# Transposing the half block, pairing two attends, reversing tiles and a shorter ring in a sparse attention with gated FFN

## The chip, the cores and the metric

One core of a Trainium2 chip. The time is the device time of one launch in microseconds (us), the median of the runs shown. A profile is one execution recorded by the hardware profiler.

## The reference

Eight batches, eight heads, 576 tokens, head dimension 64. Scores within `tau` of a row's maximum are kept, the others leave the softmax. The result, 512 columns wide, goes through a feed-forward layer of width 1024 with a convolution over three neighbouring tokens as its gate.

```python
scores = scale * np.matmul(q, k.transpose(0, 1, 3, 2))
thresh = np.max(scores, axis=-1, keepdims=True) - tau
scores = np.where(scores >= thresh, scores, -1000000000.0)
attn = np.exp(scores - np.max(scores, axis=-1, keepdims=True))
attn = attn / (np.sum(attn, axis=-1, keepdims=True) + 1e-09)
x = np.matmul(attn, v)                  # heads side by side: (8, 576, 512)
h = np.maximum(x @ w_in, 0.0)           # (8, 576, 1024)
conv_out[s] = sum(conv_w[k] * h[s + k - 1] for k in range(3))
gate = 1.0 / (1.0 + np.exp(-conv_out))
out = h * gate @ w_out                  # (8, 576, 512)
```

All is float32. The weights `w_in`, `w_out` and `conv_w` come as 64-bit words.

## The kernel before

**Tiles.** Heads go in four pairs a batch. The 576 query rows of a batch are five tiles: four of 128 rows and one half tile of 64. A *chunk* is two tiles (0, 1) or three (2, 3, 4) of a batch, so there are 16 chunks, 64 combinations of chunk and head pair, and 160 units (a unit is one tile of one pair).

**A unit** (`unit`, L421) computes scores into PSUM (`ps_s`): for batches after the first with full rows and q and k each split into a high and a low float32r part (L449, all 128 rows of the array); for the first batch, and for the half tiles of every batch, in plain float32 with the array cut into halves by rows (L442). In a half tile both heads share the 128 partitions. DVE takes the row maximum (L457) and masks and sums (L466), ACT takes the exponential (L463), small instructions on DVE or POOL work out threshold and inverse (L460, L483, L487, L490), and POOL normalizes (L495). The result is `em`, 128 x 1152, in four buffers.

**Transposes** (`transposes`, L500) turn `em` block by block on TensorE into `ps_t` (L519, two PSUM buffers); ACT copies it to `eT` (L514, one buffer). 576 keys are four blocks of 128 and a half block of 64. For full tiles the half blocks of both heads are one block of 128 columns. For a half tile the half block is done by `halves` (L532): two matmuls against parts of the identity, each for one head, which put head 0 on partitions 0 to 63 and head 1 on 64 to 127 (L534).

**Attend** (`attend`, L562) multiplies `eT` by v for one pair, two heads at a time, each on half of the array's columns (L571), into `pa`, which takes a buffer of the tag `ps_t` as the transposes do. ACT and DVE copy it as high and low part to `x` (L579, L582).

**FFN** (`ffn`, L677). `mm1` (L588) does one eighth of the hidden width for a chunk (L600), then ReLU, the three taps (L618, L627), tanh and gate (L634), and writes the result in two parts to a ring of 640 tokens. `mm2` (L656) multiplies 128 tokens of the ring by `w_out` (L665). The work of a chunk's `mm1` and of the `mm2` of the tokens that were finished by the chunk before is spread over the units of the next chunk; one `mm2` alternates with two `mm1`.

**Order.** Nothing is issued in program order. `Plan.op` collects every instruction group with an engine, a price in ns, what it reads and writes, and a rank (the unit's number less an `ahead`). `Plan.run` simulates the engines with those prices, `LATENCY` between engines and `SWITCH` between kinds of matmul ("rows", "cols", "turn", "full"), and issues for each engine the ready group of lowest rank; TensorE may stay with a kind that costs under 50 ns to follow within `KEEP` ranks. A group with `other` may go to another engine when its own has more than `BACKLOG` ready; there it is ranked `ALT` later. The buffers of a tag are handed out in the order in which the program made them. The order so found is fixed in the kernel: each engine and SP's queue of loads run it strictly in turn.

**Weights** are loaded and taken apart (`split`, L295) over the first some twenty units, at a pace set by `WRATE`.

Of the kernel before, what the change touches and what calls it, by code (L numbers as in the profile page):

```python
# [61 lines left out]
class Plan:  # L62
# [13 lines left out]
    def op(self, engine, ns, fn, w=(), r=(), ahead=0.0, other=None, kind=None):  # L76
# [12 lines left out]
        bufs = {x[0] for x in (*w, *r)}  # L89
        for x in bufs:  # L90
            x.left += 1
        self.ops.append((((engine, ns), *(other or ())), self.rank - ahead, fn if other is not None else lambda e: fn(), before, bufs, kind))

    def run(self):
# [28 lines left out]
        while events:  # L123
            t = events[0][0]
            while events and events[0][0] <= t:
                _, _, kind, x = heapq.heappop(events)
                if kind == "ready":
                    i, e = x
                    if taken[i] is None:
                        heapq.heappush(ready[e], (self.ops[i][1] + (0.0 if e == self.ops[i][0][0][0] else ALT), i))  # L130
                        if e == self.ops[i][0][0][0]:
                            load[e] += self.ops[i][0][0][1]
                elif kind == "release":
                    live.discard(x)
                elif kind == "done":
                    engine = taken[x]
                    for j in after[x]:
                        waits[j] -= 1
                        for e in came[j]:
                            late = 0.0 if e == engine == "pe" else LATENCY[engine] + (30.0 if e == "pool" != engine else 0.0)  # L140
# [66 lines left out]
def tile_tau_attention_gated_ffn(  # L207
# [54 lines left out]
    op("sp", 100, lambda: nc.sync.dma_start(tau_sb[:], tau.broadcast_to([P, 1])), w=[(tau_sb, 0)], ahead=100.0)  # L262
# [19 lines left out]

    def act(n, psum=False):
        return n * 0.833 + (170 if psum else 200)

    def dve(n, fixed=140):
        return n * 1.1 + fixed

    def pool(n):
        return n * 2.1 + 240  # L290

    def pool1(n):
        return n * 1.69 + 80

    def split(src, n, name, high, low, hr, lr, queue="sp"):  # L295
# [37 lines left out]
        op(queue, 450, load, w=[hi, lo], ahead=w + (AHEAD["load"] if queue == "sp" else 90))  # L333
        op("act", act(n), f0, w=[a], r=[hi], ahead=w)
        op("pool", n * 1.69 + 80, f1, w=[a], ahead=w, other=[("dve", 150 + n * 0.65)])
        op("dve", 150 + n * 0.55, f2, w=[a], ahead=w)
        op("dve", 150 + n * 1.1, f3, w=[a], r=[hi], ahead=w)
        op("dve", 150 + n * 1.1, f4, w=[a], r=[lo], ahead=w)
# [32 lines left out]
    RING = 5 * P  # L371
# [10 lines left out]
    def prep_rows(i, b, p, o, w, tag):  # L382
# [4 lines left out]
        op("sp", 450, lambda: nc.sync.dma_start(k[:], kp[b, p]), w=[(k, 0)], ahead=a + 2)  # L387
        op("sp", 450, lambda: nc.sync.dma_start(q[:], qd[b, p, :, :, o:o + w]), w=[(q, 0)], ahead=a + 2)
        op("act", act(2 * w), lambda: nc.scalar.activation(q[:], q[:], AF.Copy, scale=0.125), w=[(q, 0)], ahead=a)
        return k, q  # L390

    def prep_k(b, p, j, ks):
# [3 lines left out]
        op("sp", 820, lambda: nc.sync.dma_start(xk[:, :S], kd[b, p, :, j]), w=[(xk, 0)], ahead=a + 2)  # L396
# [7 lines left out]
    def prep_q(i, b, p, j, q1, q2):  # L404
# [4 lines left out]
        op("sp", 455, lambda: nc.sync.dma_start(xq[:], qd[b, p, :, j, o:o + w]), w=[(xq, 0)], ahead=a + 2)  # L409
# [6 lines left out]
    def load_v(i, b, p):  # L416
        vt = plan.buf(wk, "v", 2, [P, NBLK + 1, D], F32, f"v_{i}")
        op("sp", 820, lambda: nc.sync.dma_start(vt[:], vc[b, p]), w=[(vt, 0)], ahead=AHEAD["prep"])
        return vt

    def unit(u, k, q1, q2, o, n):  # L421
# [9 lines left out]
        tiny = [("pool", 290)]  # L431
        for h, js in enumerate(heads):
# [26 lines left out]
            def limit(e, nm=nm, th=th):  # L459
                engines[e].tensor_scalar(few[:rows, th], few[:rows, nm], -1.0, tau_sb[:rows], op0=ALU.mult, op1=ALU.subtract)  # L460
# [4 lines left out]
            def mask(ps=ps, th=th, view=view, total=total):  # L465
# [6 lines left out]
                "pe", 480 if q2 is None else 532, mm, w=[(ps, 0)],  # L472
                r=[(k, 0), (q1, 0)] if q2 is None else [(x, h) for x in (k, q1, q2)], ahead=a, kind="rows" if q2 is None else "full"
            )
            op("dve", 748, top, w=[(few, ("nm", h))], r=[(ps, 0)], ahead=a)
            op("act", 742, exp, w=[(em, h)], r=[(ps, 0), (few, ("nm", h))], ahead=a)
            op("dve", 200, limit, w=[(few, ("th", h))], r=[(few, ("nm", h)), (tau_sb, 0)], ahead=a, other=tiny)
            op("dve", 890, mask, w=[(em, h), (few, ("sum", h))], r=[(ps, 0), (few, ("th", h))], ahead=a)
# [10 lines left out]
        op("dve", 170, guard, w=[(few, "inverse")], r=ss, ahead=a, other=tiny)  # L489
        op("dve", 160, lambda: nc.vector.reciprocal(few[:rows, inverse], few[:rows, inverse]), w=[(few, "inverse")], ahead=a)  # L490
        op("dve", 165, even, w=[(few, "shift")], r=ss, ahead=a, other=tiny)
        for h in range(m):
            def norm(e, h=h):
                sl = em[:rows, h * S:(h + 1) * S]
                engines[e].tensor_scalar(sl, sl, few[:rows, 6 + h:7 + h], few[:rows, 8 + h:9 + h], op0=ALU.mult, op1=ALU.add)  # L495

            op("pool", 905, norm, w=[(em, h)], r=[(few, "inverse"), (few, "shift")], ahead=a, other=[("dve", 490)])
        return em

    def transposes(u, ems, tiles, eT):  # L500
# [4 lines left out]
        def group(i, reads, parts, *evacs):  # L505

            pt = plan.buf(ps_t, "ps_t", 2, [P, 512], F32, f"ps_t_{u}_{i}")
            width = sum(w for w, _, _ in evacs)
            op(
                "pe", max(width, 140) * 0.86, lambda: parts(pt), w=[(pt, 0)], r=reads + [(ident, 0)], ahead=AHEAD["t"], kind="turn"  # L510
# [7 lines left out]
        def turn(pt, at, em, b):  # L518
            nc.tensor.transpose(out=pt[:, at:at + P], in_=em[:, b * P:(b + 1) * P], identity=ident[:])  # L519
# [11 lines left out]

        def halves(pt, at):  # L532
            for j in range(2):
                nc.tensor.matmul(  # L534
                    pt[j * D:(j + 1) * D, at:at + n], lhsT=em[:, 4 * P:4 * P + D], rhs=ident[:, j * n:(j + 1) * n], start=True, stop=True
                )

# [10 lines left out]
        full = [x for x in ems if x[1] == P]  # L548
# [11 lines left out]
        group(8, [(x[0], 1) for x in full] + ([(em, 0)] if n < P else []), odd, *parts)  # L560

    def attend(i, eT, vt, w, x, off):  # L562
        pa = plan.buf(ps_t, "ps_t", 2, [P, 512], F32, f"pa_{i}")
        parts = [x for x in plan.wrote if x[0] is eT]
        for r in range(5):
# [10 lines left out]
            op("pe", w * 4 / 2.4 + 20, mm, w=[(pa, 0)], r=parts + [(vt, 0)], ahead=AHEAD["a"], kind="cols")  # L576
# [11 lines left out]
    def mm1(c, f, xs):  # L588
# [8 lines left out]
        for cb in range(NCB):  # L597
# [8 lines left out]
            op("pe", an * 3 / 2.4 + 40, mm, w=[(ph, 0)], r=ws + [(xs[cb], i) for i in (0, 1, 2) if i < 2 or a0], kind="full")  # L606
# [17 lines left out]
        op("pool", pool1(kn), tap0, w=[(t, 0)], r=[(hp, 0), (cw, 0)], other=[("dve", dve(kn / 2, 130))])  # L624
        for k in (0, 2):
# [5 lines left out]
            op("dve", dve(kn, 300), tap, w=[(t, 0)], r=[(hp, 0), (hp, 1), (cw, 0)])  # L631
# [24 lines left out]
    def mm2(m):  # L656
# [5 lines left out]
        for f in range(NFB):  # L662
# [8 lines left out]
            op("pe", 695, mm, w=[(po, 0)], r=gs + [(w, (f, i)) for w in w2 for i in range(0, DO, WN)], kind="full")  # L671
        op("act", act(DO, True), lambda: nc.scalar.activation(ot[:, :DO], po[:], AF.Copy), w=[(ot, 0)], r=[(po, 0)])
        op("sp", 730, lambda: nc.sync.dma_start(tokens[m * P:(m + 1) * P, :], ot[:, :DO]), r=[(ot, 0)])
# [3 lines left out]
    def ffn(c):  # L677
# [8 lines left out]
        if c < EARLY:  # L686
            return first + second
        while first or second:
# [4 lines left out]
    xs = {}  # L693
    pairs = [(c, p) for c in range(len(chunks)) for p in range(NP)]
    units = [(i, t) for i in range(len(pairs)) for t in chunks[pairs[i][0]].tiles]
# [30 lines left out]
    work = []  # L726
    for now in range(len(units) + 1):
        plan.rank = float(now)
        if now < len(units):
            i, t = units[now]  # L730
            c, p = pairs[i]
            tiles, (o, w), (a0, an) = chunks[c].tiles, chunks[c].new, chunks[c].cols
# [7 lines left out]
            if t == tiles[-1]:  # L740
# [9 lines left out]
                attend(i, eT, vts[i], w, x, off)  # L750
# [65 lines left out]
```

## Time and profile before

| | |
|---|---|
| median of 3 runs | 976.28 us (975.6 to 979.25) |
| profiled execution, its own time | 977.8 us |
| its span, first to last instruction | 976.0 us |
| TensorE busy (matmul) | 925.7 us, 6368 matmuls |
| DVE, POOL, ACT busy | 804.6, 728.6, 694.8 us |
| mean granted TensorE clock | 0.990 |
| bytes moved | 87.26 MB, mean 89 GB/s |

In the lists of instructions a row has engine, line, operation, the tiles written and read, the shapes, a count, the busy time and the mean duration of one, and after the bar the idle time of the engine ahead of them with what ended it. In a timeline a row is the start, the time until the last of its merged instructions ended, engine, line and count. Matmuls overlap, so a step is read from one start to the next. In the list of waits a row has the time in all, how often, and the longest.

### The profile page before, as it was taken

The numbers are of one execution on the slowest core, as the hardware profiler recorded it, in microseconds if no ns is written. First come the engines' busy times: TensorE is split into PE (matmuls) and PEld (weight loads), VectorE is DVE, ScalarE is ACT, GpSimd is POOL, SyncE is SP. The second block draws the span as 40 slices with busy tenths as digits, with TensorE's granted clock in tenths as the row PEclk, the third lists the DMA queues.
The fourth block names the chain that finished last, engine by engine and source line by source line (L and its number), as shares of the span: only waits on it lengthen the run. The fifth ranks groups of instructions, "written<-read, shape, count | busy, mean of one in ns | idle before, by whom it ended". The sixth has DMA issues, their size and how long they took to land.

```text
span 976.0 us, 19384 instructions
## 1 busy us (share of the span) xinstructions
PE 925.7 (95%) x6368; PEld 740.6 (76%) x6368; DVE 804.6 (82%) x1926; ACT 694.8 (71%) x1508; POOL 728.6 (75%) x1175
## 2 busy tenths in 40 slices
PE   3887779999999999999999999999999999999998
PEld 2554558878888878878888788887888878887796
DVE  4889989997988887887897879897897879988443
ACT  4766778777876778767876678777876778776443
POOL 3769898876888678887886769886776877786333
PEclk9999989999999999999999999999999999999999
DMA  6344223233322133213332223223332133311000
GB/s 224 122 146 142 80 85 115 73 91 98 94 93 80 61 104 112 85 53 105 99 106 63 81 84 108 86 74 95 104 99 76 52 102 109 100 50 46 23 22 33
DMA packets 56259, 87.26 MB, mean 89 GB/s; under 512 B 13152, under 2 KB 29536, under 8 KB 56160
## 3 DMA queue, kind: packets, MB, share of 16 engines
q1 hardware_dynamic: 55728, 84.46, 28.5%
q10 hardware_dynamic: 432, 1.57, 0.5%
q8 instruction: 51, 0.84, 0.4%
q14 instruction: 48, 0.39, 0.1%
HBM read 76.57 MB, written 9.44 MB: 88 GB/s over the span
## 4 chain that ended last, share of the span: by engine, by line
PE 74%; DVE 10%; POOL 7%; issue 3%; DMA 2%; ACT 2%; SPq 0%; POOLq 0%; DVEq 0%; ACTq 0%
PE ph L600 17%; PE po L665 17%; PE pa L571 13%; PE ps_t L519 12%; PE ps_s L449 11%; PE ps_s L442 3%; DVE em L466 3%; POOL em L495 3%; DMA q<-in_qd_dram 2%; DVE few L457 2%; POOL gl L280 2%; DVE t L627 1%; DVE t L634 1%; POOL t L618 1%; PE ps_t L534 1%
## 5 line engine op out<-in xcount | busy, mean ns | idle before, releaser
L495 POOL TENSOR_SCALAR em<-em,few 128x576 f32<-128x576 f32 x288 | 263.5, 922 | 42.4 <-DVE few L490 29.3
L466 DVE SCALAR_TENSOR_TENSOR em<-ps_s,few,em 128x576 f32<-128x576 f32 x288 | 230.1, 811 | 36.3 <-ACT em L463 30.2
L457 DVE TENSOR_REDUCE few<-ps_s 128x1 f32<-128x576 f32 x288 | 212.9, 750 | 56.1 <-PE ps_s L449 39.4
L600 PE MATMUL ph<-x,w1h 128*128 128x322 f32 (+1 forms) x1024 | 251.8, 309 | 0.9 <-ACT hp L615 0.6
L463 ACT ACTIVATE em<-ps_s,few 128x576 f32<-128x576 f32 x288 | 209.0, 740 | 42.0 <-DVE few L457 31.5
L514 ACT ACTIVATE eT<-ps_t 128x512 f32<-128x512 f32 (+2 forms) x384 | 193.8, 532 | 48.0 <-PE ps_t L519 44.8
L519 PE MATMUL ps_t<-ident,em 128*128 128x128 f32 x1280 | 191.5, 279 | 12.0 <-POOL em L495 8.1
L627 DVE SCALAR_TENSOR_TENSOR t<-hp,cw,t 128x255 f32<-128x255 f32 (+1 forms) x256 | 176.6, 693 | 29.8 <-POOL t L618 28.1
L519 PEld LDWEIGHTS ps_t<-ident,em 128*128 128x128 f32 x1280 | 148.9, 142 | 52.3 <-POOL em L495 17.4
L600 PEld LDWEIGHTS ph<-x,w1h 128*128 128x128 f32 x1024 | 177.5, 190 | 7.9 <-issue 3.9
L571 PE MATMUL pa<-eT,v 128*64 128x256 f32 (+1 forms) x1280 | 171.5, 415 | 0.0
L449 PE MATMUL ps_s<-ks,q 128*128 128x288 f32 x896 | 159.4, 306 | 7.8 <-DVE em L466 3.2
L600 PE MATMUL ph<-x,w1l 128*128 128x322 f32 (+1 forms) x512 | 152.1, 297 | 0.0
L449 PEld LDWEIGHTS ps_s<-ks,q 128*128 128x128 f32 x896 | 131.2, 189 | 23.3 <-issue 7.4
L571 PEld LDWEIGHTS pa<-eT,v 128*64 128x64 f32 x1280 | 87.1, 138 | 67.3 <-issue 7.5
L280 POOL TENSOR_TENSOR gl<-t,gh 128x321 fp32r<-128x321 f32 (+13 forms) x184 | 119.3, 660 | 12.2 <-ACT gh L644 10.6
L665 PE MATMUL po<-w2h,gh 128*128 128x512 f32 x288 | 118.4, 411 | 0.0
L665 PE MATMUL po<-w2h,gl 128*128 128x512 f32 x288 | 113.7, 395 | 2.2 <-POOL gl L280 2.2
L665 PE MATMUL po<-w2l,gh 128*128 128x512 f32 x288 | 113.3, 393 | 0.0
L618 POOL TENSOR_SCALAR t<-hp,cw 128x321 f32<-128x321 f32 (+1 forms) x128 | 71.9, 562 | 38.2 <-ACT hp L615 31.3
L600 PEld LDWEIGHTS ph<-x,w1l 128*128 128x128 f32 x512 | 97.3, 190 | 0.3
L280 POOL TENSOR_TENSOR ks<-xk,ks 64x576 fp32r<-64x576 f32 x56 | 81.7, 1460 | 16.5 <-ACT ks L398 10.2
(56 smaller groups left out, 1127.6 us busy)
## 6 DMA issues: line engine op xcount, KB each, us to landing
v<-in_vc_dram SPq DMA_DIRECT2D x64, 320.0 KB, 3.0
xk<-in_kd_dram SPq DMA_DIRECT2D x56, 288.0 KB, 2.9
xq<-in_qd_dram SPq DMA_DIRECT2D x112, 128.0 KB, 2.3
k<-in_kp_dram SPq DMA_DIRECT2D x36, 320.0 KB, 3.1
out_dram<-ot SPq DMA_DIRECT2D x36, 256.0 KB, 2.0
stage<-in_w_out_dram SPq DMA_DIRECT2D x8, 512.0 KB, 3.4
stage<-in_w_in_dram SPq DMA_DIRECT2D x5, 512.0 KB, 4.1
q<-in_qd_dram SPq DMA_DIRECT2D x28, 64.0 KB, 3.2
```

Of the source, the lines that this page charges most:

```text
L280: engines[e].tensor_tensor(dst, x, y, op=ALU.subtract)
L449: nc.tensor.matmul(ps[:, c, :CH], lhsT=q[:, h, o:o + n], rhs=k[:, h, c * CH:(c + 1) * CH], start=(i == 0), stop=(i == 1))
L457: nc.vector.tensor_reduce(few[:rows, nm], ps[:rows, :, :CH], op=ALU.max, axis=mybir.AxisListType.XY, negate=True)
L463: nc.scalar.activation(view(), ps[:rows, :, :CH], AF.Exp, bias=few[:rows, nm])
L466: nc.vector.scalar_tensor_tensor(view(), ps[:rows, :, :CH], few[:rows, th], view(), op0=ALU.is_ge, op1=ALU.mult, accum_out=few[:rows, total])
L495: engines[e].tensor_scalar(sl, sl, few[:rows, 6 + h:7 + h], few[:rows, 8 + h:9 + h], op0=ALU.mult, op1=ALU.add)
L514: "act", act(w, True), lambda dst=dst, src=src: nc.scalar.activation(dst(), src(pt), AF.Copy),
L519: nc.tensor.transpose(out=pt[:, at:at + P], in_=em[:, b * P:(b + 1) * P], identity=ident[:])
L571: nc.tensor.matmul(pa[j * D:(j + 1) * D, :w], lhsT=vt[:, blk + j, :], rhs=eT[:, blk, :w], start=(r == 0), stop=(r == 4))
L600: nc.tensor.matmul(ph[:, :an], lhsT=w1[w][:, cb, fs], rhs=xs[cb][:, h, :an], start=(cb == 0 and i == 0), stop=(cb == NCB - 1 and i == 2))
L627: nc.vector.scalar_tensor_tensor(t[:, :kn], hp[:, k:kn + k], cw[:, 3 * f + k:3 * f + k + 1], t[:, :kn], op0=ALU.mult, op1=ALU.add)
L665: nc.tensor.matmul(po[:], lhsT=x[:, f, at:at + P], rhs=w[:, f, :], start=(f == 0 and i == 0), stop=(f == NFB - 1 and i == 2))
```

## The change

- **Half block as a transpose.** `halves` goes. The last group of a chunk's pair transposes columns 448 to 575 of the half tile's `em` as one block more (`turn(..., 3.5)`); the keys wanted lie on partitions 64 to 127 of the result, and two ACT copies of 64 x 64 take them to `eT`, one for each head.
- **v for two pairs.** From chunk 3 on (`JOINT = 3`) the attend of an even pair waits for that of the odd pair behind it: both are issued when the parts of both are there. `eT` has two buffers.
- **Tiles in reverse** for each odd pair (`order`), so that half tiles of two pairs are neighbours.
- **Ring of 512 tokens** in place of 640. In `ffn` all `mm2` of the chunk before stand ahead of the `mm1`.
- **Start.** The first k is loaded from ACT's queue ahead of its weight loads, the first q heads SP's queue; q of the first batch is scaled in two instructions.
- The threshold is taken with a negated `tau` and may go to ACT too, as may the normalization.
- **The planner's numbers:** `AHEAD`, `LATENCY`, `SWITCH`, `KEEP`, `ALT`, `BACKLOG`, `WRATE` and most prices, those of loads by their size; a group may have a delay of its own (`late`).

```diff
-AHEAD = {'s': 6.0, 't': 3.5, 'a': 3.5, 'prep': 4.0, 'w': 2.0, 'load': 4.25}
-LATENCY = {"pe": 197.0, "act": 145.0, "dve": 130.0, "pool": 115.0, "sp": 2000.0}
+AHEAD = {'s': 6.0, 't': 3.25, 'a': 3.0, 'prep': 4.0, 'w': 2.75, 'load': 4.75}
+LATENCY = {"pe": 210.0, "act": 145.0, "dve": 110.0, "pool": 75.0, "sp": 2000.0}
-MOE = (2, 1)
-BACKLOG = {'pool': 28000.0, 'dve': 500.0, 'act': 9000000000.0}
-WRATE = (0.891, 1.015)
-ALT = 3.0
+MOE = (2, 2)
+BACKLOG = {'pool': 28000.0, 'dve': 343.0, 'act': 9000000000.0}
+WRATE = (0.891, 0.894)
+ALT = 12.0
...
-    "rows": {"cols": 190, "turn": 240, "full": 290}, "cols": {"rows": 230, "turn": 260, "full": 310},
-    "turn": {"rows": 95, "cols": 95, "full": 85}, "full": {"rows": 95, "cols": 95, "turn": 5},
+    "rows": {"cols": 145, "turn": 155, "full": 200}, "cols": {"rows": 205, "turn": 155, "full": 205},
+    "turn": {"rows": 195, "cols": 145, "full": 5}, "full": {"rows": 195, "cols": 145, "turn": 0},
 }
-KEEP = 1.2
+JOINT = 3
+KEEP = 2.352
...
-    RING = 5 * P
+    RING = 4 * P
...
-        op("sp", 450, lambda: nc.sync.dma_start(k[:], kp[b, p]), w=[(k, 0)], ahead=a + 2)
-        op("sp", 450, lambda: nc.sync.dma_start(q[:], qd[b, p, :, :, o:o + w]), w=[(q, 0)], ahead=a + 2)
+        if i:
+            op("sp", sp(S + D), lambda: nc.sync.dma_start(k[:], kp[b, p]), w=[(k, 0)], ahead=a + 2)
+        else:
+            op("act", 450, lambda: nc.scalar.dma_start(k[:], kp[b, p]), w=[(k, 0)], ahead=210, late=sp(S + D) + LATENCY["sp"])
+        op("sp", sp(2 * w), lambda: nc.sync.dma_start(q[:], qd[b, p, :, :, o:o + w]), w=[(q, 0), (q, 1)], ahead=a + 2 + 100 * (not i))
...
-        def halves(pt, at):
-            for j in range(2):
-                nc.tensor.matmul(
-                    pt[j * D:(j + 1) * D, at:at + n], lhsT=em[:, 4 * P:4 * P + D], rhs=ident[:, j * n:(j + 1) * n], start=True, stop=True
-                )
...
         def odd(pt):
-            for i, x in enumerate(full):
-                turn(pt, i * P, x[0], 8)
-            if n < P:
-                halves(pt, w)
+            for x in full + small:
+                turn(pt, x[2], x[0], 8 if x[1] == P else 3.5)
 
         parts = [(w, lambda: eT[:, 8, :w], lambda pt: pt[:, :w])]
-        if n < P:
-            parts.append((n, lambda: eT[:, 4, off:off + n], lambda pt: pt[:, w:w + n]))
+        for _, m, at in small:
+            for j in range(2):
+                parts.append((
+                    m, lambda j=j: eT[j * D:(j + 1) * D, 4, at:at + m], lambda pt, j=j: pt[D:, w + j * m:w + (j + 1) * m]
+                ))
...
         if c < EARLY:
             return first + second
+        while len(second) > 1:
+            seq.append(second.pop(0))
         while first or second:
             seq += second[:n2] + first[:n1]
             first, second = first[n1:], second[n2:]
...
+    def order(i):
+        c, p = pairs[i]
+        return chunks[c].tiles[::-1] if p % 2 else chunks[c].tiles
...
-                eT = plan.buf(wk, "eT", 1, [P, NBLK, 320], F32, f"eT_{i}")
+                eT = plan.buf(wk, "eT", 2, [P, NBLK, 320], F32, f"eT_{i}")
...
-                attend(i, eT, vts[i], w, x, off)
+                parts = [x for x in plan.wrote if x[0] is eT]
+                waiting.append((i, eT, vts[i], w, x, off, parts))
+                if c < JOINT or p % 2:
+                    parts = [x for y in waiting for x in y[-1]]
+                    for y in waiting:
+                        attend(*y[:-1], parts)
+                    waiting = []
```

More of the change, by code (lines that the diff above doesn't have):

```diff
@@ L74, in buf, with op @@
         return b
-    def op(self, engine, ns, fn, w=(), r=(), ahead=0.0, other=None, kind=None):
+    def op(self, engine, ns, fn, w=(), r=(), ahead=0.0, other=None, kind=None, late=0.0):
         i = len(self.ops)
@@ L91, in op @@
             x.left += 1
-        self.ops.append((((engine, ns), *(other or ())), self.rank - ahead, fn if other is not None else lambda e: fn(), before, bufs, kind))
+        self.ops.append((((engine, ns), *(other or ())), self.rank - ahead, fn if other is not None else lambda e: fn(), before, bufs, kind, late))
     def run(self):
@@ L139, in run @@
                         for e in came[j]:
-                            late = 0.0 if e == engine == "pe" else LATENCY[engine] + (30.0 if e == "pool" != engine else 0.0)
+                            late = 0.0 if e == engine == "pe" else LATENCY[engine] + self.ops[x][6] + (60.0 if e in ("pool", "pe") and e != engine else 0.0)
                             came[j][e] = max(came[j][e], t + late)
@@ L331, in f4 @@
             nc.vector.scalar_tensor_tensor(v(U32), words()[0], 29, v(U32), op0=ALU.logical_shift_right, op1=ALU.bitwise_or)
-        op(queue, 450, load, w=[hi, lo], ahead=w + (AHEAD["load"] if queue == "sp" else 90))
+        if queue == "sp":
+            op("sp", sp(2 * n), load, w=[hi, lo], ahead=w + AHEAD["load"])
+        else:
+            op("act", 450, load, w=[hi, lo], ahead=90, late=sp(2 * n) + LATENCY["sp"])
         op("act", act(n), f0, w=[a], r=[hi], ahead=w)
[L335 to L338, printed above, removed]
+        op("pool", 600 * n / 512, f1, w=[a], ahead=w, other=[("dve", 150 + n * 0.65)])
+        op("dve", 70 + n * 0.53, f2, w=[a], ahead=w)
+        op("dve", 100 + n * 1.3, f3, w=[a], r=[hi], ahead=w)
+        op("dve", 100 + n * 1.3, f4, w=[a], r=[lo], ahead=w)
         op("act", act(n), lambda: nc.scalar.activation(high(), v(), AF.Copy), w=[hr], r=[a], ahead=w)
@@ L430, in unit @@
         a = AHEAD["s"]
-        tiny = [("pool", 290)]
+        tiny = [("pool", 200)]
         for h, js in enumerate(heads):
@@ L503, in transposes, with group @@
         em, n, off = ems[-1]
-        def group(i, reads, parts, *evacs):
+        def group(i, reads, parts, *evacs, width=4 * P):
             pt = plan.buf(ps_t, "ps_t", 2, [P, 512], F32, f"ps_t_{u}_{i}")
-            width = sum(w for w, _, _ in evacs)
             op(
-                "pe", max(width, 140) * 0.86, lambda: parts(pt), w=[(pt, 0)], r=reads + [(ident, 0)], ahead=AHEAD["t"], kind="turn"
+                "pe", width * 0.852, lambda: parts(pt), w=[(pt, 0)], r=reads + [(ident, 0)], ahead=AHEAD["t"], kind="turn"
             )
@@ L518, in turn @@
         def turn(pt, at, em, b):
-            nc.tensor.transpose(out=pt[:, at:at + P], in_=em[:, b * P:(b + 1) * P], identity=ident[:])
+            nc.tensor.transpose(out=pt[:, at:at + P], in_=em[:, int(b * P):int(b * P) + P], identity=ident[:])
         def turns(pt, b0):
@@ L693, in tile_tau_attention_gated_ffn @@
     xs = {}
+    def order(i):
+        c, p = pairs[i]
+        return chunks[c].tiles[::-1] if p % 2 else chunks[c].tiles
     pairs = [(c, p) for c in range(len(chunks)) for p in range(NP)]
-    units = [(i, t) for i in range(len(pairs)) for t in chunks[pairs[i][0]].tiles]
+    units = [(i, t) for i in range(len(pairs)) for t in order(i)]
     whole, last, vts = {}, {}, {}
@@ L725, in tile_tau_attention_gated_ffn @@
         load_weight(i)
-    work = []
+    work, waiting = [], []
     for now in range(len(units) + 1):
@@ L731, in tile_tau_attention_gated_ffn @@
             c, p = pairs[i]
-            tiles, (o, w), (a0, an) = chunks[c].tiles, chunks[c].new, chunks[c].cols
+            tiles, (o, w), (a0, an) = order(i), chunks[c].new, chunks[c].cols
             at, n = TILES[t]
```

79 lines of the change are left out of this document (47 added, 32 removed).

## The prediction, before the run

> **What bounds the kernel now.** I read the page's totals first, then the busy time by stage, then TensorE's waits.
>
> ```profile
> span 976.0 us, 19384 instructions
> PE 925.7 (95%) x6368; PEld 740.6 (76%) x6368; DVE 804.6 (82%) x1926; ACT 694.8 (71%) x1508; POOL 728.6 (75%) x1175
> GB/s 224 122 146 142 80 85 115 73 91 98 94 93 80 61 104 112 85 53 105 99 106 63 81 84 108 86 74 95 104 99 76 52 102 109 100 50 46 23 22 33
> ```
>
> TensorE is busy for 95% of the span, DVE for 82%. An average over the span can hide stages with other limits, so the next view cuts it (columns: PE, weight loads, DVE, ACT, POOL, granted clock, DMA share, GB/s).
>
> ```profile
> 0.00:60.00 60.00, 39.56 (x228) 23.22 (x230) 40.72 (x101) 35.09 (x64) 32.88 (x63) 0.95 0.51 166
> 60.00:180.00 120.00, 100.08 (x674) 72.80 (x673) 112.43 (x254) 89.10 (x180) 106.07 (x133) 0.94 0.36 109
> 180.00:930.00 750.00, 744.16 (x5258) 608.50 (x5257) 633.36 (x1545) 554.28 (x1225) 572.24 (x944) 1.00 0.28 84
> ```
>
> There are two stages. Up to 180 us TensorE is idle for 20.4 + 19.9 = 40 us, and from 60 us on DVE is busy for 112 of 120: weights are being split beside the first batch. From 180 to 930 us TensorE is busy for 744 of 750 us at full clock, while DVE, the next engine, has 117 us to spare. In that stage a microsecond taken off TensorE is a microsecond off the time, as long as the others keep up.
>
> ```profile
> PE ps_s L442 <- ACT q L389: 11.2, 1, 11.2
> PE ps_s L449 <- DVE em L466: 2.1, 4, 0.8
> ```
>
> The first row is TensorE's one long wait in the whole trace: its first work, waiting for the first q. The second is its largest in 180 to 930 us, 2.1 us in all. So TensorE hardly waits there, and what can go is its own work. Busy is not the same as streaming, though, and the change acts on that difference: on what it costs to pass from one shape of matmul to another.
>
> **Half block as a transpose.** The two halves (four L534 instructions) give way to one more 128-column transpose (L519). The timeline has both kinds of group:
>
> ```profile
> 575.95 1.04 PE L519 MATMUL ps_t<-ident,em 128*128 128x128 f32 x8
> 576.74 0.47 PE L665 MATMUL po<-w2h,gh 128*128 128x512 f32 x1
> 577.05 0.39 PE L665 MATMUL po<-w2h,gl 128*128 128x512 f32 x1
> ...
> 584.10 0.38 PE L519 MATMUL ps_t<-ident,em 128*128 128x128 f32 x2
> 584.41 0.34 PE L534 MATMUL ps_t<-ident,em 128*64 128x64 f32 x4
> 584.68 0.38 PE L600 MATMUL ph<-x,w1h 128*128 128x256 f32 x1
> 584.90 0.28 PE L600 MATMUL ph<-x,w1l 128*128 128x256 f32 x1
> ```
>
> Starts count here, since durations overlap. Eight transposes take 0.79 us to the next start, 0.10 each. Two transposes and the halves take 584.68 - 584.10 = 0.58. Three transposes come to 3/8 of 0.79 = 0.30; as the last of a run is the cheap one (the next matmul starts early and pays it back, 577.05 - 576.74 = 0.31, as the first step behind the halves is long too, 0.22), the truth is nearer to 0.25. Saved: 0.28 to 0.33, taken as 0.33. There are 32 such groups, 28 of them behind the first batch: 28 x 0.33 = **9.2 us**, bounds 7.8 and 9.2; the four in the first batch lie beside idle time and count nothing.
>
> By the Trainium skill (TensorE: Matmul & The Clock Gate, Part 4: PE-mode transpose) a 128x128 transpose costs about 275 ns inside a kernel; at that price the saving would be near 0.16 a group and 4.5 us in all. The duration in the row agrees with that figure, but the step between starts is 0.10, and the step is what TensorE pays.
>
> On ACT one copy of 128x64 becomes two of 64x64, which no row shows; the nearest is the 128x64 copy, quoted below at 236 ns. 32 x 0.24 = 7.6 us more at most on an engine with 196 us free between 180 and 930; hidden, and 7.6 us if not.
>
> **v for two head pairs at a time.** From the fourth chunk on, 13 chunks x 4 pairs = 52 attends become 26 double ones. What does one visit to attend cost beyond its columns?
>
> ```profile
> 500.65 1.23 PE L449 MATMUL ps_s<-ks,q 128*128 128x288 f32 x8
> 501.72 0.38 PE L519 MATMUL ps_t<-ident,em 128*128 128x128 f32 x2
> ...
> 503.86 0.31 PE L600 MATMUL ph<-x,w1l 128*128 128x322 f32 x1
> 504.01 0.31 PE L600 MATMUL ph<-x,w1h 128*128 128x322 f32 x1
> 504.25 2.38 PE L571 MATMUL pa<-eT,v 128*64 128x256 f32 x20
> 506.56 1.35 PE L449 MATMUL ps_s<-ks,q 128*128 128x288 f32 x8
> 507.74 1.04 PE L519 MATMUL ps_t<-ident,em 128*128 128x128 f32 x8
> ```
>
> ```profile
> 569.62 0.28 PE L600 MATMUL ph<-x,w1h 128*128 128x256 f32 x1
> 569.83 0.72 PE L442 MATMUL ps_s<-k,q 64*64 64x288 f32 x8
> 570.47 0.39 PE L600 MATMUL ph<-x,w1h 128*128 128x256 f32 x1
> 570.69 0.28 PE L600 MATMUL ph<-x,w1l 128*128 128x256 f32 x1
> 570.82 0.28 PE L600 MATMUL ph<-x,w1h 128*128 128x256 f32 x1
> 571.02 2.91 PE L571 MATMUL pa<-eT,v 128*64 128x320 f32 x20
> 573.87 0.66 PE L519 MATMUL ps_t<-ident,em 128*128 128x128 f32 x4
> ```
>
> The attend of 256 columns takes 506.56 - 504.25 = 2.31 us, that of 320 takes 573.87 - 571.02 = 2.85: 8.4 ns a column, so 2.16 of the 2.31 is columns. From 504.01 to 507.74 are 3.73 us; take off one step of L600 (0.15, 503.86 to 504.01), the columns and eight score matmuls (1.07, 500.65 to 501.72), and 0.35 is left for the visit: 0.09 going in, 0.15 inside, 0.11 behind. A second attend on the heels of the first saves that. I take 0.32, since a transpose behind the attend loses less than a score: 26 x 0.32 = **8.3 us**. It needs the second attend to follow at once; its PSUM buffer of tag ps_t should be free, because both attends wait for all copies out of ps_t. If something steps between them the saving is nothing.
>
> What it adds is a wait: the double attend takes both ps_t buffers, and the next pair's transposes wait for ACT's and DVE's copies of pa. Behind a waiting transpose in TensorE's queue stands everything else, so the order must put other work there; scores, mm1 and mm2 are that work, and eT now has two buffers. Taken as +2 us, up to the second rival's price below.
>
> **Reversed tiles.** The half tiles of two neighbouring pairs come one after the other. Visit to L442: 569.62 to 570.82 is 1.20 us, of which three steps of L600 are 3 x 0.13 = 0.39 (570.69 to 570.82) and the columns, at the attend's rate per pair, 288 x 2 x 0.84 ns = 0.48; 0.33 remains. 7 batches x 2 = 14 joined visits: 14 x 0.33 = **4.6 us**, zero if other work steps between. The half tile's loads of k and q in every second pair are wanted two tiles sooner; they are asked for six tiles ahead, and I cost that at nothing.
>
> **Start.** The first k goes from SP's queue to the front of ACT's, ahead of three weight loads; the first q goes to the front of SP's, past tau and conv_w; q is scaled by halves.
>
> ```profile
> 2.10 8.36 DMA q<-in_qd_dram
> 11.16 2.32 PE ps_s L442 x8
> stage<-in_w_in_dram ACTq DMA_DIRECT2D x3, 512.0 KB, 6.7
> out_dram<-ot SPq DMA_DIRECT2D x36, 256.0 KB, 2.0
> ```
>
> Now q lands after 8.4 us, behind a k and beside weights. With k and q (576 KB) in front, at the page's 224 GB/s, they need 2.6 us plus the 2.0 us that an unhindered load takes to land; from an issue near 0.7 that is about 5.5, and with the scaling the first score starts near 6.5 in place of 11.2. The weights behind k come 1.4 us later. Of these 4.7 us I carry **4**, since DVE and POOL then limit until 180 us and both start earlier; bounds 0 and 4.7.
>
> **mm2 ahead of mm1, ring of 512.** All mm2 of a chunk stand ahead of its eight mm1, which now come as a block.
>
> ```profile
> L627 DVE SCALAR_TENSOR_TENSOR t<-hp,cw,t 128x321 f32<-128x321 f32 x128 | 92.3, 727 | 15.6 <-POOL t L618 14.6 <-POOL hp L610 0.4 <-POOL hp L612 0.4
> L634 DVE SCALAR_TENSOR_TENSOR t<-t,hp 128x321 f32<-128x321 f32 x64 | 41.1, 643 | 3.5 <-ACT t L636 3.3
> L514 ACT ACTIVATE eT<-ps_t 128x64 f32<-128x64 f32 x32 | 7.5, 236 | 0.0
> L579 ACT ACTIVATE x<-pa 128x320 fp32r<-128x320 f32 x32 | 14.0, 436 | 21.8 <-PE pa L571 21.5
> L582 DVE TENSOR_TENSOR x<-pa,x 128x320 fp32r<-128x320 f32 x32 | 15.6, 488 | 5.8 <-ACT x L579 4.9
> ```
>
> One mm1 of 322 columns costs DVE 2 x 0.727 + 0.643 = 2.10 us and TensorE 12 x 0.15 = 1.80. A bare block of eight leaves TensorE 2.4 us short, over seven or eight such chunks at most 19 us; but tiles run between, and now too each chunk ends with several mm1 in a row without a visible wait. Taken as +2. The ring is shorter than a batch, so mm1's writes must wait for old tokens to be read; with the mm2 ahead in the queue that is met: nothing, or the same 2.4 us a chunk if a read comes late.
>
> **Other costs of the planner** (latencies, prices, KEEP from 1.2 to 2.352, later diversion of small work). They reorder all queues and remove no work. Bounds: TensorE's 40 idle us before 180 could shrink; in the long stage there are only 6 us of idle time to win, but any amount to lose. I take zero.
>
> **Sum.** 9.2 + 8.3 + 4.6 + 4 - 2 - 2 = 22 us off the profiled execution's 977.8 (span 976.0 and 1.8 around it). That execution stands 1.5 above the median of 976.28; off the median: **954 us**.
>
> **Rivals.** *Only the half block and the start pay.* If the paired attends and half tiles are parted in the queue, or their savings return as small waits, 9.2 + 4 - 4 = 9 us stay: 967, up to no change. For it: joins need two chains to end together; against: both attends depend on the same last copies.
>
> *Slower: DVE starves at the joins.* While a double attend runs (2 x 2.31 us or more) and pa is copied out (0.436 + 0.488), no transpose empties an em tile; when all four em tiles are full, DVE has no scores to work on. A full loss is 4.6 + 0.9 = 5.5 us at 26 joins. DVE has 117 us to spare, 95 once TensorE is 22 shorter: from 95 / 26 = 3.7 us lost at each join DVE sets the end. At 5 us the stage lasts 633 + 130 = 763 instead of 750; with the start's 4 back the time is 985. Against it: mm1 gives DVE other work; for it: mm2, which gives DVE nothing, now stands in blocks.
>
> *More gain: the new order also fills the start.* DVE was free for 27 of the first 180 us. With 6.5 unavoidable, up to 20 us are there, 4 of them counted: 16 more would give 938.
>
> **Chances.** Forecast (940 to 966) 0.50; parted joins 0.17, of which 0.10 within 0.5% of before (what a measurement of this kernel can tell from no change); starved DVE 0.20; fuller start 0.13. So faster 0.70, same 0.10, slower 0.20. The range 934 to 984 leaves out a little of the two outer cases. Were the slower case set aside, the forecast's own range would be 940 to 966.
>
> **What would show it.** In the changed profile: no matmul with 64 output columns writing ps_t; pa in runs of 40 matmuls, 20 only in the early chunks; L442's successor in runs of 16 for the half tiles; the first score near 6.5 us; in the long stage TensorE as busy as now and the stage 20 us shorter. I am wrong if TensorE's idle time there rises from 6 to over 20 us, with waits for POOL's em or ACT's eT at the transposes, or if pa still comes in twenties.

## Result: 4% slower

The changed kernel takes 1015.4 us (median of 4 runs, 1014.2 to 1017.1) against 977.8 of the kernel before (4 runs): ratio 1.0386, 95% interval 1.0354 to 1.0419. The profiled execution took 1017.1 us, its span is 1015.0.

The totals of the changed page, and below them busy time by stage (PE, weight loads, DVE, ACT, POOL, clock, DMA share, GB/s):

```profile
span 1015.0 us, 19203 instructions
PE 934.6 (92%) x6272; PEld 752.4 (74%) x6272; DVE 812.6 (80%) x1982; ACT 704.9 (69%) x1568; POOL 706.6 (70%) x1116
...
PE 40%; DVE 32%; POOL 12%; ACT 8%; issue 7%; DMA 1%; SPq 0%; ACTq 0%; POOLq 0%; DVEq 0%
```

The last row gives the shares of the chain that ended last. Before it was:

```profile
PE 74%; DVE 10%; POOL 7%; issue 3%; DMA 2%; ACT 2%; SPq 0%; POOLq 0%; DVEq 0%; ACTq 0%
```

The stages of the changed kernel:

```profile
0.00:60.00 60.00, 44.79 (x260) 26.04 (x261) 47.94 (x114) 39.73 (x80) 36.02 (x61) 0.94 0.54 180
60.00:180.00 120.00, 101.89 (x691) 75.07 (x689) 115.39 (x264) 94.08 (x202) 108.30 (x147) 0.96 0.35 104
180.00:930.00 750.00, 708.43 (x4849) 585.53 (x4849) 607.87 (x1521) 535.33 (x1199) 529.52 (x848) 0.98 0.28 82
930.00:1015.00 85.00, 79.47 (x480) 65.71 (x476) 41.35 (x86) 35.72 (x88) 32.77 (x61) 0.98 0.08 27
```

In the long stage TensorE is idle for 42 of 750 us where it was idle for 6, yet no other engine is fuller: DVE, ACT and POOL all do less than before in these 750 us. No engine has become the bound; all four wait for each other. On the chain DVE went up from 10% to 32%, TensorE down from 74% to 40%. The granted clock of the stage fell from 1.00 to 0.98, but a run shown below loses as much there at 1.00, so the clock is not the cause.

Two places are the same work in both kernels: the twelfth attend (the end of chunk 2) and the last one. Before:

```profile
182.36 2.38 PE L571 MATMUL pa<-eT,v 128*64 128x256 f32 x20
...
922.17 2.91 PE L571 MATMUL pa<-eT,v 128*64 128x320 f32 x20
```

Changed (the last row is a pair of attends):

```profile
176.08 2.38 PE L590 MATMUL pa<-eT,v 128*64 128x256 f32 x20
...
956.28 5.60 PE L590 MATMUL pa<-eT,v 128*64 128x320 f32 x40
```

The twelfth attend starts 6.3 us earlier. By the start of the next instruction after the last attend (925.01 before, 961.82 changed) 37 us have been lost: some 43 us in the stage between. So the loss is in the long stage, the one in which the prediction had TensorE bound, and the start is a gain.

TensorE's waits in the changed kernel, the longest first:

```profile
PE ps_t L544 <- DVE x L601: 25.1, 21, 2.3
PE ps_s L461 <- DVE em L488: 10.8, 9, 2.9
PE ps_t L544 <- POOL em L521: 9.2, 10, 1.8
PE ps_s L468 <- DVE em L488: 8.6, 16, 1.2
PE ps_s L461 <- ACT q L408: 6.5, 1, 6.5
```

And those of all engines:

```profile
ACT t L655 <- DVE t L646: 72.2, 77, 2.4
DVE x L601 <- ACT x L598: 56.9, 26, 4.5
POOL few L482 <- DVE few L476: 55.4, 25, 6.6
...
POOL t L637 <- ACT hp L634: 49.9, 35, 8.8
```

Before, these rows read:

```profile
POOL few L460 <- DVE few L457: 27.9, 27, 2.5
ACT t L636 <- DVE t L627: 13.9, 29, 1.7
DVE x L582 <- ACT x L579: 9.1, 19, 1.3
```

The first row of the first list looks like the rival of the starved DVE: after a double attend, transposes wait for DVE's copy of `pa` (L601). DVE in turn stands idle 57 us in front of that copy, up to 4.5 us at a join. But ACT also waits 72 us for the FFN's taps (L646; 13.9 us before, where the line is L627), which have nothing to do with joins.

### The profile page after: what moved, and what is told of

Same layout as the page of the kernel before. It is cut to its first block, busy times and chain, and to the rows that moved or that the text cites. A ratio compares the mean times of both kernels' runs of the same rounds, so it can differ in the third digit from the quotient of the medians.

```text
span 1015.0 us, 19203 instructions
## 1 busy us (share of the span) xinstructions
PE 934.6 (92%) x6272; PEld 752.4 (74%) x6272; DVE 812.6 (80%) x1982; ACT 704.9 (69%) x1568; POOL 706.6 (70%) x1116
## 4 chain that ended last, share of the span: by engine, by line
PE 40%; DVE 32%; POOL 12%; ACT 8%; issue 7%; DMA 1%; SPq 0%; ACTq 0%; POOLq 0%; DVEq 0%
PE po L684 13%; DVE t L646 9%; PE ps_t L544 8%; DVE em L488 8%; PE ps_s L468 6%; PE pa L590 6%; DVE few L476 5%; PE ph L619 5%; POOL em L521 4%; DVE t L653 4%; ACT em L485 3%; POOL gl L285 2%; DVE few L505 2%; POOL t L637 2%; PE ps_s L461 1%
## 5 line engine op out<-in xcount | busy, mean ns | idle before, releaser
L521 POOL TENSOR_SCALAR em<-em,few 128x576 f32<-128x576 f32 x288 | 258.2, 903 | 73.8 <-DVE few L512 42.6
L544 PE MATMUL ps_t<-ident,em 128*128 128x128 f32 x1312 | 200.3, 286 | 41.0 <-DVE x L601 25.1
L646 DVE SCALAR_TENSOR_TENSOR t<-hp,cw,t 128x255 f32<-128x255 f32 (+1 forms) x256 | 190.1, 746 | 36.3 <-POOL t L637 31.6
L539 ACT ACTIVATE eT<-ps_t 128x512 f32<-128x512 f32 (+2 forms) x416 | 201.2, 507 | 21.9 <-PE ps_t L544 19.7
L544 PEld LDWEIGHTS ps_t<-ident,em 128*128 128x128 f32 x1312 | 156.9, 146 | 73.7 <-DVE x L601 21.7
L468 PE MATMUL ps_s<-ks,q 128*128 128x288 f32 x896 | 167.8, 313 | 12.1 <-DVE em L488 8.6
L590 PE MATMUL pa<-eT,v 128*64 128x256 f32 (+1 forms) x1280 | 164.8, 411 | 0.4 <-ACT eT L539 0.4
L285 POOL TENSOR_TENSOR gl<-t,gh 128x255 fp32r<-128x255 f32 (+9 forms) x192 | 127.5, 676 | 14.5 <-ACT gh L663 12.6
L637 POOL TENSOR_SCALAR t<-hp,cw 128x321 f32<-128x321 f32 (+1 forms) x128 | 75.6, 591 | 61.5 <-ACT hp L634 49.9
L655 ACT ACTIVATE t<-t 128x321 f32<-128x321 f32 (+1 forms) x128 | 57.0, 445 | 79.5 <-DVE t L646 72.2
```

What stands on the lines that cost most here:

```text
L285: engines[e].tensor_tensor(dst, x, y, op=ALU.subtract)
L468: nc.tensor.matmul(ps[:, c, :CH], lhsT=q[:, h, o:o + n], rhs=k[:, h, c * CH:(c + 1) * CH], start=(i == 0), stop=(i == 1))
L521: engines[e].tensor_scalar(sl, sl, by, to, op0=ALU.mult, op1=ALU.add)
L539: "act", act(w, True), lambda dst=dst, src=src: nc.scalar.activation(dst(), src(pt), AF.Copy),
L544: nc.tensor.transpose(out=pt[:, at:at + P], in_=em[:, int(b * P):int(b * P) + P], identity=ident[:])
L590: nc.tensor.matmul(pa[j * D:(j + 1) * D, :w], lhsT=vt[:, blk + j, :], rhs=eT[:, blk, :w], start=(r == 0), stop=(r == 4))
```

## The experiments

All are medians of runs taken side by side with the kernel before, whose median was 978.9 to 979.8 in these comparisons. Three theories stood at first: **J**, the double attends; **M**, the block of `mm2` ahead of `mm1`; **N**, the planner's new numbers. The block of `mm2` comes with the ring of 512 and a second `eT` buffer, and M stands for the three together. J and M had an argument each from the profile; N was the part that the prediction had set to zero.

### The half block alone

The kernel before, with `halves` replaced as in the change.

> The kernel before with nothing but the half block as a transpose. By the prediction's price (0.33 us a group, 28 groups that count) 9 us less than before, about 968. If the transpose pays what its duration says (0.27 us) about 972. If the two copies on ACT in place of one matter, no change or slower.

Measured: 974.9, ratio 0.9962 (0.9948 to 0.9975). A gain, but of 3.7 us, not 9. From the twelfth attend to the last the trace has 733.8 us in place of 740.3, so 6.5 of the 9.2 came in the stage where they were expected; the start was 2.8 us longer, at a granted clock of 0.87 between 60 and 180 us in place of 0.94 (why is not shown). The same group of transposes as in the prediction now reads

```profile
584.84 0.49 PE L518 MATMUL ps_t<-ident,em 128*128 128x128 f32 x3
585.08 0.36 PE L595 MATMUL ph<-x,w1h 128*128 128x256 f32 x1
```

and takes 0.24 us to the next start in place of 0.58. The price of the group, 0.33, is right, and not the 0.16 that the duration of a transpose gave; of the 2.7 us that are missing in the stage, 1.8 are idle time of TensorE between 180 and 930 us (7.7 in place of 5.8).

### Single attends

```diff
-JOINT = 3
+JOINT = 99
```

> The changed kernel with each attend on its own (JOINT = 99), all else as changed. Theory J (the double attend holds both PSUM buffers of ps_t, and transposes wait for the copies of pa): most of the loss is gone, 965 to 985. Theory N (the planner's new numbers give an order that does not fit the engines): it stays near 1005 to 1015. Theory M (mm2 in a block, then mm1 in a block): it stays near 1000 to 1015.

Measured: 1014.4, ratio 1.0357 (1.0334 to 1.0379). J falls. In 180 to 930 us TensorE waits for the copies of `pa` only half as long, 12.3 us in place of 24.6,

```profile
PE ps_t L544 <- DVE x L601: 12.3, 13, 1.9
PE ps_s L468 <- DVE em L488: 12.1, 28, 1.0
```

and the time is the same. The longest wait in the list was a place where lateness came out, not where it came from.

### The planner's numbers put back

```diff
-AHEAD, LATENCY, SWITCH, KEEP, ALT, BACKLOG, WRATE and every price as changed
+the same of before
```

> The changed kernel with the planner's numbers of before (AHEAD, LATENCY, SWITCH, KEEP, ALT, BACKLOG, WRATE and all prices), the structure as changed. Theory N: 955 to 970. Theories J and M: 1000 to 1020, since double attends and the block of mm2 are still there.

Measured: **964.5**, ratio 0.9847 (0.9828 to 0.9867). The whole structure of the change, under the old numbers, is 14 us faster than the kernel before; the numbers cost 51.

### Single attends, ring of 640, mm2 alternating with mm1

```diff
-MOE = (2, 2)
+MOE = (2, 1)
...
-JOINT = 3
+JOINT = 99
...
-    RING = 4 * P
+    RING = 5 * P
...
-        while len(second) > 1:
-            seq.append(second.pop(0))
...
-                eT = plan.buf(wk, "eT", 2, [P, NBLK, 320], F32, f"eT_{i}")
+                eT = plan.buf(wk, "eT", 1, [P, NBLK, 320], F32, f"eT_{i}")
```

> The changed kernel with single attends, one eT buffer, the ring of 640 and one mm2 alternating with two mm1 as before; half block as transpose, reversed tiles, start and the planner's numbers as changed. Theory M: clearly faster than the run with single attends alone, by 20 us or more. Theory J: within 5 us of that run. Theory N: still about 1005.

Measured: 996.3, ratio 1.0176 (1.0155 to 1.0197). That is 18 us less than with single attends alone: under the new numbers M (block, ring and buffer together) has a share, below the 20 that its theory asked for; a later run asks whether it has one under the old.

### Only the numbers, in the old structure

> The kernel before with the constants and prices as changed, its structure untouched (halves, single attends, ring of 640, tiles in order, the first k on SP). If the numbers cost the time whatever the structure: 1000 to 1025. If they only do harm together with double attends and the block of mm2: 970 to 985.

Measured: 1024.7, ratio 1.0462 (1.0447 to 1.0478). Halves, single attends, ring of 640 and order of tiles untouched, and 45 us slower. Its long stage looks like that of the changed kernel, at a granted clock of 1.00:

```profile
180.00:930.00 750.00, 709.27 (x4896) 568.45 (x4892) 601.74 (x1484) 524.33 (x1160) 537.88 (x870) 1.00 0.27 82
```

So N holds, and needs none of the structure.

### Prices or constants

**P**: the prices of instruction groups. **C**: the constants (`AHEAD`, `LATENCY`, `SWITCH`, `KEEP`, `ALT`, `BACKLOG`, `WRATE`).

> The changed kernel with the prices of instruction groups of before, and with the constants (AHEAD, LATENCY, SWITCH, KEEP, ALT, BACKLOG, WRATE) as changed. Theory P (the new prices are too low for what DVE does, so that the order fixed at planning is too tight and each queue stands behind a late copy or tap): about 965. Theory C (the constants give a bad order): 1000 to 1015.

Measured: 973.1, ratio 0.9950 (0.9932 to 0.9967).

> The changed kernel with the constants AHEAD, LATENCY, SWITCH, KEEP, ALT, BACKLOG and WRATE of before and the new prices. Theory P: 1000 to 1015. Theory C: about 965. If both have a share, both this and the run with old prices lie between.

Measured: 1027.7, ratio 1.0492 (1.0468 to 1.0515). It is the prices. The constants of before under the new prices make it 12 us worse, which neither theory expected.

### Which prices

What do the groups really take? From the changed trace, the mean time from one start to the next, over those cases in which the next one followed at once:

| group | price before | new price | mean step |
|---|---|---|---|
| row maximum, DVE | 748 | 668 | 668 |
| mask, DVE | 890 | 738 | 738 |
| exponential, ACT | 742 | 625 | 634 |
| tap of 321 / 255 columns, DVE | 653 / 581 | 493 / 423 | 623 / 722 |
| guard, DVE | 170 | 112 | 284 |
| normalization, POOL | 905 | 807 | 885 |

The first three new prices are within 2% of the step. The last three are below it, and nearer to what the instruction takes when it is alone: beside an idle POOL 14 taps of 321 columns step by 463 ns and the guard by 75, and the normalization steps by 817 where no tap or gate runs beside it. Two rows of DVE and two of POOL from the changed timeline:

```profile
589.94 1.49 DVE L646 SCALAR_TENSOR_TENSOR t<-hp,cw,t 128x255 f32<-128x255 f32 x1
...
597.10 1.41 DVE L505 TENSOR_SCALAR few<-few 128x2 f32<-128x2 f32 x1
```

```profile
589.73 1.41 POOL L285 TENSOR_TENSOR ks<-xk,ks 64x576 fp32r<-64x576 f32 x1
...
596.92 1.56 POOL L285 TENSOR_TENSOR ks<-xk,ks 64x576 fp32r<-64x576 f32 x1
```

An instruction of 128 x 2 elements, priced at 112 ns, lasts 1.41 us, from just after a POOL instruction began until that one ended (598.5); a tap priced at 423 lasts 1.49 beside another. Over the whole trace, the 27 taps that POOL (its memsets not counted) ran beside for less than a tenth of their time took 522 ns in the mean, the 201 with POOL beside them for over 60% took 792; the guard 162 and 505; the mask, which reads its scores from PSUM, 813 and 809. Not every instruction on SBUF is slowed: the reciprocal of 128 x 2 elements takes 164 and 162. The Trainium skill (SBUF — State Buffer, "SBUF: two separate sides") says that VectorE and GpSimd share one pair of ports as an exclusive lock: whoever starts first holds it for the whole instruction, and for VectorE that concerns instructions with two SBUF inputs or in a two-port mode. Taps have two SBUF inputs and the mask one, and the trace agrees. The planner has no such lock; a price is all it can know of it.

Two runs split the prices along that line, and one takes DVE's FFN alone (**P1**: what matters are prices below what the engine does; **P2**: any reserve helps).

```diff
 def dve(n, fixed=...): n * 1.07 + 65   ->  n * 1.1 + 140      # gate, copies
 taps: dve(kn, 150)                     ->  dve(kn, 300)
```

> The changed kernel with only DVE's prices for the FFN and copies put back (taps 653 in place of 493 ns, gate 493 in place of 408; the changed trace shows taps 0.52 to 0.61 us from start to start in the median and 0.62 to 0.72 in the mean). Theory P, if these are the prices that matter: 965 to 985. Theory C: 1005 to 1015.

Measured: 995.3, ratio 1.0167 (1.0152 to 1.0182): 20 us of the loss, from the taps, the gate and the copies; it lies between the two ranges.

```diff
 the same, and POOL: n * 2.2 + 140 -> n * 2.1 + 240, first tap n * 0.9 + 225 -> n * 1.69 + 80,
 normalization 807 -> 905; limit, guard, reciprocal, even: 125, 112, 82, 124 -> 200, 170, 160, 165
```

> The changed kernel with the prices of before for all of POOL, for DVE's FFN work and copies and for the small instructions of DVE and POOL (those whose steps in the changed trace are longer than the new price: taps 0.62 to 0.72 us in the mean against 0.49, normalization 0.89 against 0.81, guard 0.28 against 0.11); the row maximum, mask, exponential, ACT, TensorE and loads keep the new prices. Theory P1 (the harm is in the prices that are below what the engine does): about 975. Theory P2 (every group needs slack, whatever it really takes): near 995, as with the FFN's prices alone.

Measured: **962.6**, ratio 0.9826 (0.9811 to 0.9840), the best of all and 12 us better than its theory asked for.

```profile
180.00:930.00 750.00, 738.96 (x5187) 616.29 (x5187) 637.73 (x1582) 563.46 (x1282) 558.11 (x886) 1.00 0.28 83
```

```profile
DVE x L601 <- ACT x L598: 43.8, 19, 3.9
...
ACT t L655 <- DVE t L646: 33.3, 41, 2.2
```

TensorE's idle time in the long stage falls from 42 to 11 us. DVE still stands 44 us in front of the copies of `pa`, so that starving is there and costs little; the wait for taps is halved. In this trace the prices fit the mean steps, other than that of the guard: taps 653 and 581 ns against 679 and 598, normalization 905 against 909, guard 170 against 273.

> The rest of the prices put back instead: row maximum, mask, exponential, ACT, TensorE, DVE's part of the weights, loads, and the extra delay into POOL and TensorE. In the changed trace the new prices of these are the real steps (0.668, 0.738, 0.63 us). Theory P1: 1005 to 1020. Theory P2: about 990.

Measured: 1005.4, ratio 1.0259 (1.0242 to 1.0276). This is the other half of the prices, and it gives 10 of the 53 us; why it gives any, the runs don't show.

> The changed kernel with only POOL's prices of before (normalization 905 in place of 807, splits, first tap, small work on POOL). DVE's FFN prices alone gave 20 of the 52 us that all shared prices give. If POOL's prices carry the rest, about 983; if DVE's small instructions carry it, near 1012; if the gain needs both sides right, anything near 1010 with the sum missing.

Measured: 992.9, ratio 1.0142 (1.0122 to 1.0162). POOL's prices give 22 us, DVE's FFN 20, all shared ones 53: both sides carry it; the remaining 10 us belong to DVE's small instructions or to having all of them right, which these runs don't part. None of the three expectations fits. Each price put back also makes another order, so shares of 10 to 20 us are not sure one by one. The division by shared prices is: the six kernels here that have all the new ones take 996 to 1028 us, the eleven with the old ones 963 to 990, whatever the constants, the attends and the order of tiles.

> The run with shared prices of before, those prices raised by 30 per cent (normalization 1177 ns, taps 849 and 754, guard 221), so above what the trace shows in the mean. Theory P1 as accuracy (a price should be the time under contention): 975 to 1000. As slack (any reserve on DVE and POOL does it): 955 to 967.

Measured: 999.0, ratio 1.0204 (1.0186 to 1.0222). Prices 30% higher are 36 us worse. In this trace taps step by 629 and 645 ns and the normalization by 897, far below the raised prices. So reserve is not what helps; the best run is the one whose prices lie near the steps beside the other engine. A price between the two was not tried.

### The parts of the structure under prices that fit

```diff
 all numbers of before, and JOINT = 3 -> 99
```

> The run with all numbers of before, but each attend on its own. By the prediction's price (26 visits at 0.32 us) 8 us slower than that run's 964.5, about 973. If the double attends cost as much by the wait for ps_t as they save: 964. If they cost more: 955 to 962.

Measured: 970.8, ratio 0.9926 (0.9904 to 0.9947): the double attends are worth 6.3 us.

```diff
-        return chunks[c].tiles[::-1] if p % 2 else chunks[c].tiles
+        return chunks[c].tiles
```

> The run with all numbers of before, but with the tiles of each pair in order. By the prediction's price (14 joined visits at 0.33 us) 4.6 us slower than that run's 964.5, about 969. If the reversal gains nothing: 964.

> The run with shared prices of before (962.6), tiles in order. By the prediction's price of the joined half tiles 4.6 us more, 967. If the 25 us that the order of tiles cost under all old numbers lie in the structure: 985 to 990.

> All numbers of before, single attends and tiles in order. If order and double attends do not bear on each other: 970.8 + 25 = 996. If tiles in order only do harm together with double attends: 971 to 977.

Measured: 989.8 (ratio 1.0100, 1.0083 to 1.0116), 976.7 (0.9975, 0.9964 to 0.9986) and 986.4 (1.0079, 1.0064 to 1.0095). Against the same kernels with reversed tiles (964.5, 962.6, 970.8) the order of tiles is worth 25, 14 and 16 us, and none of the three fits an expectation. Runs of 16 matmuls for two half tiles, 12, 15 and 15 with reversal, fall to none; at 0.33 us the visits so added explain 4 to 5 us. The rest stays open. It does not need the double attends, as the third pair shows. With tiles in order the structure under old numbers is 7 to 10 us slower than the kernel before, half block included: some other part of it costs time that the reversal takes back, and these runs don't say which.

> All numbers of before, single attends, one eT buffer, ring of 640 and one mm2 alternating with two mm1; half block as transpose, reversed tiles and the start as changed. If the block of mm2 costs 18 us whatever the prices (as between the second and the fourth run, 1014.4 to 996.3): 953. If it costs little once the prices fit, as the prediction took it (2 us): 966 to 973.

Measured: 967.8, ratio 0.9903 (0.9873 to 0.9932), against 970.8 with the block of `mm2`: 3 us, within the spread of its runs (963.9 to 970.4). The 18 us of M came with the new numbers and are not there with the old ones.

> The run with shared prices of before, with the constants of before as well. If the new constants help with prices that fit: 965 to 975. If the constants of before are as good: 958 to 964.

Measured: 975.8, ratio 0.9966 (0.9953 to 0.9979), against 962.6 with the new constants, just above the first range. So the new constants gain 13 us with the shared prices put back, gain 12 with the new prices, and lose 9 with all old prices (973.1 against 964.5). Here the constants had no worth of their own, apart from the prices they ran with.

## Why the prediction was wrong

**The step that failed** is "Other costs of the planner", taken as zero because those numbers "reorder all queues and remove no work". The same sentence had the bound right: 6 us of idle time to win in the long stage, "but any amount to lose". The loss was there: 45 us in the old structure, 51 in the new one. In the new structure it came from the prices of DVE's and POOL's shared work, the main ones of which lie below the steps that these engines take beside each other: 53 us are gained when they alone are put back. The prediction compared the new prices with nothing, though the profile of before had what was needed: its rows give 727 ns as the mean of a tap of 321 columns, which the new price puts at 493. Overlap accounts for some 70 ns of that, as between 811 and 738 for the mask, not for 234. The sign that the prediction set for being wrong did appear (TensorE idle for 42 us in the long stage, over 20), but the longest wait at the transposes was for DVE's copies of `pa`, not for POOL's `em` or ACT's `eT`.

**The slower rival** named a real wait, DVE idle at the joins, and gave it a threshold of 3.7 us a join; 56.9 us over 26 waits is 2.2. By its own figures it could not set the end, its full price led to 985, and single attends (1014.4) showed that it did not. The chance of 0.20 for a slower kernel stood on this rival: the prediction had a slower end in view, but for another reason.

**Start**: the first score came when forecast, the 4 us behind it are not shown. k and q are now issued first on two queues,

```profile
0.71 0.38 ACTq L402 DMA_DIRECT2D k<-in_kp_dram  x1
...
6.00 0.72 ACT L408 ACTIVATE q<-q 128x256 f32<-128x256 f32 x2 [3.38 <-DMA q<-in_qd_dram]
```

```profile
6.47 2.29 PE L461 MATMUL ps_s<-k,q 64*128 64x288 f32 x8 [6.47 <-ACT q L408]
```

and the first score starts at 6.47 (forecast 6.5, before 11.16). The twelfth attend is 6.3 us earlier; four were carried. But this hangs on the planner's numbers too. With the new start under all old numbers the first score starts at 9.60 and the twelfth attend (180.75) is 1.6 us earlier; with the new numbers alone the first score is no earlier (11.26) and the twelfth attend (178.40) still gains 4.0. So the two terms do not part, and the match with the forecast is in part luck. The 2.0 us taken for an unhindered load came from a row of stores (`out_dram<-ot`); the shortest row of loads before has 2.3.

**Half block**: the mechanism and the price of a group were right (0.58 to 0.24 us), that all of it reaches the end was not. 9.2 forecast, 6.5 measured between the twelfth attend and the last, 3.7 in the median.

**Double attends**: 8.3 less 2 for the new wait forecast, 6.3 measured under numbers that fit. All 26 stand in runs of 40 matmuls in the changed trace, and the half tiles behind the first batch in 14 runs of 16, so the rival of the parted joins did not occur.

**Reversed tiles**: 4.6 forecast, 14 to 25 measured. The price of the visit was not the larger part of it.

**mm2 ahead of mm1**: a cost of 2 forecast, 3 measured with ring and buffer, under old numbers and within the spread.

Together: with shared prices that fit, the change is 17 us faster than the kernel before (962.6 against 979.8 in that comparison); the forecast was 22. That the sum comes so near is luck in part: the reversal gave three to five times its term, and with tiles in order the same parts under old numbers end 10 us above the kernel before.

## What to carry to other kernels

Where one program fixes the order of all queues, its prices are part of the kernel: check each against the step in the trace, under the load it will run in, before pricing anything else in a change. An instruction that is slowed by another engine needs its time beside that engine, neither the time alone nor a reserve on top: too low cost 53 us here, 30% too high 36. When engines all become emptier and all wait for each other, as here, the longest wait need not be the cause; put whole groups of numbers back before testing it.

## What the runs showed of the hardware that was not expected

A DVE instruction on 128 x 2 elements took up to 1.41 us where its median is 0.17, and taps took 792 ns in place of 522, while POOL worked beside them; the mask, with its main input in PSUM, was not touched (813 and 809). And the order of tiles alone moved this kernel by 14 to 25 us with the same instructions to run, several times what the prediction had for it (4.6).
